# Low parts of the weights on VectorE alone, item 0's products in another order, an earlier start of the decoding, and the spare loop inside a conditional

## The chip, the cores and the metric

One core of a Trainium2 chip runs the whole program. The metric is the device time of one execution in microseconds, as the median of several runs. Engines are named as the profile names them: PE (TensorE), PEld (its weight loads), DVE (VectorE), ACT (ScalarE), POOL (GpSimd), SP (SyncE, which here issues the DMAs of weights).

## What is computed

Three layers follow each other: a block-sparse attention, a mixture of eight experts of which every token takes one, and a gated feed-forward block.

```python
x = attn(q, k, v)                       # (1536, 512): 2 x 768 tokens, 8 heads of 64
logits = x @ w_gate + modality_bias[modality_id]
e_idx = argmax(logits, axis=1)          # one of E = 8 experts for each token
for e in range(E):
    mask = e_idx == e
    h = maximum(x[mask] @ w1[e], 0.0)   # w1[e]: 512 x 1024
    out[mask] = gate_w[mask] * (h @ w2[e])   # w2[e]: 1024 x 512
g = out @ g2w                           # 512 x 1536
y = (silu(g) * (out @ v2w)) @ o2w       # o2w: 1536 x 512
```

The matrices of the feed-forward block come as 64-bit floating point numbers, all others as 32-bit.

## The kernel before

**Products in three parts.** Every float32 operand of a large product is written as a high part (float32 rounded to the format that PE multiplies, an ACT copy) and a low part (the operand minus its high part, a subtraction). `mm3` multiplies high by high, low by high and high by low: three matmuls, lines 802 to 804. For a weight tile, `split_w` makes both parts: line 788 on ACT makes `wh`, line 789 on the engine `eng` makes `wl`. A weight tile is 128x1024 (512 KB), and there are 8 for each item of work: four of w1 (`hidden`) and four of w2 (`project`).

**Items.** Tokens are sorted by expert on the chip, and the experts' work is cut into five items of fixed size, `KIND = "TQSQP"`: 3, 4, 1, 4 and 2 blocks of 128 tokens. Each item takes 4 steps with w1 and 4 with w2, and in each step the split of the tile three steps ahead (`WB`) is issued first, and the raw load of the tile three beyond that (`RB`). Both the raw tiles and the parts have three buffers: a raw tile's buffer comes free when its `wl` has been made, a part's buffer when the matmuls with it are done. Experts with more tokens than their item holds would go through a spare loop at line 1324, which runs `n_over` times.

**Who makes `wl`.** A list `DVES` (line 903) gives VectorE every second tile of item 0 and of the item of one block; the rest goes to POOL. In all, POOL makes 32 of the 40 tiles and VectorE 8.

**Item 0** runs while the routing of the later items is worked out on VectorE with many short instructions (`route`, `route_where`, `route_items`). Lines 1086 to 1113 fix the order by hand. PSUM has banks T (3), S (2), P (1) and V (2). `hidden` puts each half of its result in a T bank, ACT makes its high part `hh` (line 819) and VectorE its low part `hl` (line 822), which frees the bank. The low parts of `hidden_0(2)` are held back (`later`) until the routing of item 1 is done.

**Decoding.** The 64-bit weights are decoded on VectorE with five integer instructions for each half tile (lines 1200 to 1210, 128x512), then split: ACT makes the high part (line 1219), POOL the low part (line 1220). `decode` is a generator, and `bg_step(n)` runs n of its steps between other work. The first six halves are started at item 3 (`j == NS - 2`), the others inside the feed-forward block, which needs 36 in all.

All engines work through their instructions in the order of the program; nothing is reordered at run time.

Of the kernel before, what the change touches and what calls it, by code (L numbers as in the profile page):

```python
# [7 lines left out]
F32 = mybir.dt.float32  # L8
F32R = mybir.dt.float32r
BF16 = mybir.dt.bfloat16  # L10
I32 = mybir.dt.int32
ACTF = mybir.ActivationFunctionType
ALU = mybir.AluOpType
# [6 lines left out]
def sparse_attention_moe_swiglu_kernel(  # L20
# [45 lines left out]
    IT = 256  # L66
# [24 lines left out]
    def bank(tag):  # L91
        t = ps.tile([128, 512], F32, tag=tag, bufs=BANKS[tag], name="ps_" + tag)
        return t
# [709 lines left out]
        nc.tensor.matmul(out=out_, lhsT=ah, rhs=bl, start=False, stop=False)  # L803
        nc.tensor.matmul(out=out_, lhsT=al, rhs=bh, start=False, stop=stop)  # L804

    def hidden(c, x, w, later=None):
        n = x[0].shape[2]
        hh = pl["h"].tile([128, 2, n], F32R, tag="hh", name="hh")
        hl = pl["h"].tile([128, 2, n], F32R, tag="hl", name="hl")
        per = 512 // n  # L810
        for f0 in range(0, 2, per):
            p = bank("T")[:, 0:per * n].rearrange("p (f c) -> p f c", f=per)
            for f in range(f0, f0 + per):
                sl = slice(128 * f, 128 * f + 128)
                for kk in range(KD):
                    mm3(p[:, f - f0, :], w[0][:, kk, sl], w[1][:, kk, sl], x[0][:, kk, :], x[1][:, kk, :], kk == 0,
                        kk == KD - 1)
            fs = slice(f0, f0 + per)
            nc.scalar.activation(out=hh[:, fs], in_=p, func=ACTF.Relu)  # L819

            def low(p=p, fs=fs):
                nc.vector.scalar_tensor_tensor(out=hl[:, fs], in0=p, scalar=0.0, in1=hh[:, fs].bitcast(F32),  # L822
                                               op0=ALU.max, op1=ALU.subtract)

            if later is None:
                low()
            else:
                later.append(low)
        return hh, hl
# [69 lines left out]
    n_load = [0]  # L899
    n_split = [0]  # L900


    DVES = [i for i, (wn, j, c) in enumerate(preps) if (KIND[j] == "S" or i < 2 * NC1) and i % 2]

    def load_to(n):
        while n_load[0] < min(n, len(preps)):
            wn, j, c = preps[n_load[0]]
# [5 lines left out]
    def split_to(n, limit=None):  # L913
        limit = len(preps) if limit is None else limit
        while n_split[0] < min(n, limit):
            key = preps[n_split[0]]
            load_to(min(n_split[0] + RB, limit))
            ready[key] = split_w(pl["wc"], loaded.pop(key), nc.vector if n_split[0] in DVES else nc.gpsimd)
            n_split[0] += 1
        load_to(min(n_split[0] + RB, limit))  # L920

# [152 lines left out]
    split_to(2, 2 * NC1)  # L1074
    st_x(NT - 1)

    def hidden_0(c, later=None):
        split_to(c + WB, 2 * NC1)
        hs.append(hidden(c, x, ready.pop(("w1", 0, c)), later))

    def project_0(c, split=True):
        if split:
# [16 lines left out]
    adv(6)  # L1099
    for fn in later:  # L1100
        fn()
    hidden_0(3)
    yp = [y_banks(CT, "S")]
    project_0(0, False)
    while rg:
        adv(1000)
    xs = gather(pl["xg"], *idx_of(1))
    rg.append(route_items(2, NI))
    project_0(1)
    adv(6)  # L1110
    scale_x(xs)
    while rg:
        adv(1000)
    attn.close()
# [78 lines left out]
    def decode(wn, fb, i, pool):  # L1193
        r = r64.pop((wn, fb, i))
        shape = list(r.shape)
        w32 = r.bitcast(I32).rearrange("p a (b two) -> p a b two", two=2)
        lo, hi = w32[:, :, :, 0], w32[:, :, :, 1]
        a = dec_p.tile(shape, I32, tag="da", name="da")
        b = dec_p.tile(shape, I32, tag="db", bufs=1, name="db")
        nc.vector.tensor_scalar(out=a, in0=hi, scalar1=0x7FFFFFFF, scalar2=None, op0=ALU.bitwise_and)  # L1200
        nc.vector.tensor_scalar(out=b.bitcast(F32), in0=a.bitcast(F32), scalar1=T_LO, scalar2=T_HI, op0=ALU.max,
                                op1=ALU.min)
        yield
        nc.vector.tensor_scalar(out=a, in0=b, scalar1=3, scalar2=0x3FFFFFF8, op0=ALU.logical_shift_left,
                                op1=ALU.bitwise_and)
        yield
        nc.vector.scalar_tensor_tensor(out=b, in0=lo, scalar=29, in1=a, op0=ALU.logical_shift_right,  # L1207
                                       op1=ALU.bitwise_or)
        yield
        nc.vector.scalar_tensor_tensor(out=a, in0=hi, scalar=-2 ** 30, in1=b, op0=ALU.bitwise_and,  # L1210
                                       op1=ALU.bitwise_or)
        load64()
        yield
        if i == 0:
            whole = [128, 2, DM] if wn == "o" else [128, KD, 256]
            fw[wn, fb] = [pool.tile(whole, F32R, tag=wn + x, name=wn + x) for x in "hl"]
        part = (slice(None), slice(i, i + 1)) if wn == "o" else (slice(None), slice(None), slice(128 * i, 128 * i + 128))
        wh, wl = (t[part] for t in fw[wn, fb])
        nc.scalar.activation(out=wh, in_=a.bitcast(F32), func=ACTF.Copy)  # L1219
        nc.gpsimd.tensor_tensor(out=wl, in0=a.bitcast(F32), in1=wh.bitcast(F32), op=ALU.subtract)  # L1220

    def bg_step(n=1):
        while n and bg:
# [3 lines left out]
            except StopIteration:  # L1227
                bg.pop(0)

    store_y(0, yp[0], slice(0, CT), slice(0, CT))  # L1230
    yp.append(y_banks(CT, "T"))
    project_0(2)
    x = split_of(1, xs)
    project_0(3)
    store_y(1, yp[1], slice(0, CT), slice(0, CT))
    sexc = route_starts()

    def before(j):

        return min(NTOK, sum(128 * BLOCKS[kd] for kd in KIND[:j]))  # L1240

    done = 2 * NC1
    late = None
    for j in range(1, NS):
# [4 lines left out]
        n = 128 * BLOCKS[kd]  # L1249
        if not last:  # L1250
            xs = gather(pl["xg"], *idx_of(j + 1))
        if j == NS - 2:
            bg += [decode(wn, 0, i, fw_p) for wn in "gvo" for i in range(2)]
            load64()
            load64()
        hs, h1 = [], []
        for c in range(NC1):
            split_to(done + WB)
            w = ready.pop(("w1", j, c))
            if kd != "S":  # L1260
                hs.append(hidden(c, x, w))
            else:
                h1.append(hidden1(c, x, w))
                if c > 1:
                    hs.append(turn_h1(h1[c - 2]))
            if c == 0 and late is not None:
                store_y1(*late)
                late = None
            if c == NC1 - 1 and not last:
                scale_x(xs)  # L1270
            if c == 1 and j == 2:
                sorted_tokens(*tok_rows)
            bg_step(2)
            done += 1
        if last:
            break
# [2 lines left out]
        for c in range(NC1):  # L1279
            split_to(done + WB)  # L1280
            w = ready.pop(("w2", j, c))
            if c == 0 and kd == "S":
                yp = bank("S")
            elif c % 2 == 0 and kd != "S":
                yp = y_banks(n, "T" if c else "S")
            if kd != "S":
                project(c, hs, w, yp)
                if c % 2:
                    store_y(c // 2, yp, bass.ds(sa, n), bass.ds(sd, n))
            else:  # L1290
                project1(c, hs, w, yp)
                if c == 0:
                    hs += [turn_h1(h) for h in h1[2:]]
            bg_step(2)
            done += 1
            if c == 1:
                x = split_of(j + 1, xs)
            if c == 2 and j == 1:
                tok_rows = sorted_rows(sexc)
# [7 lines left out]
    for tag, d0, cols in (("S", 0, (0, 1)), ("S", 2, (0,)), ("V", 3, (1,))):  # L1307
        nd = len(cols)
        yp = bank(tag).rearrange("p (d c) -> p d c", d=2)[:, 0:nd]
        for c in (0, 1) if d0 == 0 else (2, 3):  # L1310
            if c not in ws:
                split_to(done + WB)
                done += 1
                ws[c] = ready.pop(("w2", NS - 1, c))
            project(c, hs, ws[c], [yp] * (1 if nd == 2 else 2), cols)
            bg_step(2)
        ds = slice(d0, d0 + nd)
        nc.scalar.activation(out=yh[:, ds, bass.ds(sa, IT)], in_=yp, func=ACTF.Copy)
        nc.vector.tensor_tensor(out=yl[:, ds, bass.ds(sd, IT)], in0=yp, in1=yh[:, ds, bass.ds(sd, IT)].bitcast(F32),
# [1 line left out]
    bg_step(100)  # L1321


    with tc.For_i(0, n_over, 1) as it:
        ii = pl["xg"].tile([128, 2], I32, tag="ii", name="ii")
        nc.vector.tensor_copy(out=ii, in_=idx[:, bass.ds(it * NB + NB * NS, 2)])
        e = nc.sync.value_load(tab[0:1, 0, bass.ds(it + NS, 1)], min_val=0, max_val=E - 1)
        xo = gather(pl["xg"], ii[:, 0:1], ii[:, 1:2])
        scale_x(xo)
        xo = split_x(pl["xg"], xo)  # L1330
        hs = [hidden(c, xo, split_w(pl["wc"], load_w(pl["raw"], e, "w1", c), nc.vector)) for c in range(NC1)]
        sa = nc.scalar.value_load(tab[0:1, 1, bass.ds(it + NS, 1)], min_val=0, max_val=NTOK)
        sd = nc.vector.value_load(tab[0:1, 1, bass.ds(it + NS, 1)], min_val=0, max_val=NTOK)
        for c in range(NC1):
            if c % 2 == 0:
                yp = y_banks(IT, "S")
            project(c, hs, split_w(pl["wc"], load_w(pl["raw"], e, "w2", c), nc.vector), yp)
            if c % 2:
                store_y(c // 2, yp, bass.ds(sa, IT), bass.ds(sd, IT))
    moe.close()  # L1340


# [88 lines left out]
```

## Time and profile before

| | us |
|---|---|
| median of 3 runs | 624.97 (623.2 to 626.79) |
| profiled execution, its own time | 623.85 |
| its span, first to last instruction | 622.1 |
| PE busy in the span | 575.0 (92%) |
| DVE busy | 381.9 (61%) |
| ACT busy | 212.3 (34%) |
| POOL busy | 194.5 (31%) |

The busy shares are means over stages with different limits: attention (to about 105 us), item 0 (to 163.06), items 1 to 4 (to 308.58) and the feed-forward block (from 313.98). [...]

### The profile page before, as it was taken

The numbers are of one execution on the slowest core, as the hardware profiler recorded it, in microseconds if no ns is written. First come the engines' busy times: TensorE is split into PE (matmuls) and PEld (weight loads), VectorE is DVE, ScalarE is ACT, GpSimd is POOL, SyncE is SP. The second block draws the span as 40 slices with busy tenths as digits, with TensorE's granted clock in tenths as the row PEclk, the third lists the DMA queues.
The fourth block names the chain that finished last, engine by engine and source line by source line (L and its number), as shares of the span: only waits on it lengthen the run. The fifth ranks groups of instructions, "written<-read, shape, count | busy, mean of one in ns | idle before, by whom it ended". The sixth has DMA issues, their size and how long they took to land.

```text
span 622.1 us, 9023 instructions
## 1 busy us (share of the span) xinstructions
PE 575.0 (92%) x3396; PEld 486.2 (78%) x3396; DVE 381.9 (61%) x688; ACT 212.3 (34%) x370; POOL 194.5 (31%) x252
## 2 busy tenths in 40 slices
PE   7969997977999979998689999999999999999995
PEld 6869986976888768888668888888888888888884
DVE  6557796657624654959304866947856875783333
ACT  5757844431432453344212343212121221221110
POOL 5572013215445637557400221201110210120025
PEclk8979998877999979999889999999999999999998
DMA  9999248324322637444100322212121220200013
GB/s 251 194 227 223 79 97 256 114 68 136 120 94 76 215 124 237 141 164 163 43 2 0 102 102 68 101 35 67 68 68 35 95 76 18 84 34 1 1 67 135
DMA packets 78270, 65.04 MB, mean 105 GB/s; under 512 B 25156, under 2 KB 73296, under 8 KB 78032
## 3 DMA queue, kind: packets, MB, share of 16 engines
q1 hardware_dynamic: 76144, 57.61, 32.6%
q0 software_dynamic: 2080, 6.82, 3.2%
q8 instruction: 28, 0.46, 0.3%
q14 instruction: 18, 0.15, 0.1%
HBM read 57.88 MB, written 6.35 MB: 103 GB/s over the span
## 4 chain that ended last, share of the span: by engine, by line
PE 48%; issue 1%; POOL 1%; POOLq 0%; DVE 0%
PE ps_T L802 11%; PE ps_T L804 11%; PE ps_T L803 11%; PE ps_S L803 3%; PE ps_S L802 3%; PE ps_S L804 3%; PE ps_V L804 1%; PE ps_P L802 1%; PE ps_V L803 1%; PE ps_V L802 1%; PE ps_P L803 1%; PE ps_P L804 1%; POOL out_dram L1381 1%; POOLq L1426 0%; POOL tk L1380 0%
## 5 line engine op out<-in xcount | busy, mean ns | idle before, releaser
L789 POOL TENSOR_TENSOR wl<-raw,wh 128x1024 fp32r<-128x1024 f32 x32 | 80.2, 2508 | 71.3 <-ACT wh L788 56.2
L1359 DVE TENSOR_TENSOR hv<-sg,ps_T 128x512 f32<-128x512 f32 x36 | 24.7, 686 | 83.2 <-PE ps_T L804 81.9
L802 PE MATMUL ps_T<-yh,gh 128*128 128x512 f32 x144 | 57.5, 399 | 5.4 <-issue 5.4
L1361 ACT ACTIVATE fh<-hv 128x512 fp32r<-128x512 f32 x36 | 22.8, 633 | 107.5 <-DVE hv L1359 107.5
L804 PE MATMUL ps_T<-yh,gl 128*128 128x512 f32 x144 | 57.1, 396 | 0.0
L803 PE MATMUL ps_T<-yl,gh 128*128 128x512 f32 x144 | 56.9, 395 | 0.0
L802 PE MATMUL ps_T<-yh,vh 128*128 128x512 f32 x144 | 56.8, 394 | 0.0
L804 PE MATMUL ps_T<-yh,vl 128*128 128x512 f32 x144 | 56.7, 394 | 0.0
L803 PE MATMUL ps_T<-yl,vh 128*128 128x512 f32 x144 | 56.3, 391 | 0.0
L1220 POOL TENSOR_TENSOR gl<-da,gh 128x512 fp32r<-128x512 f32 x12 | 15.6, 1302 | 127.4 <-ACT gh L1219 127.4
L802 PE MATMUL ps_T<-xh,wh 128*128 128x512 f32 (+2 forms) x128 | 47.0, 367 | 3.5 <-DVE hl L822 3.5
L804 PE MATMUL ps_T<-xh,wl 128*128 128x512 f32 (+2 forms) x128 | 46.6, 364 | 1.4 <-POOL wl L789 1.4
L788 ACT ACTIVATE wh<-raw 128x1024 fp32r<-128x1024 f32 x40 | 42.0, 1054 | 16.9 <-issue 4.0
L803 PE MATMUL ps_T<-xl,wh 128*128 128x512 f32 (+2 forms) x128 | 46.4, 363 | 0.0
L1357 ACT ACTIVATE sg<-ps_T 128x512 f32<-128x512 f32 x36 | 21.4, 594 | 59.6 <-PE ps_T L804 59.6
L1363 DVE TENSOR_TENSOR fl<-hv,fh 128x512 fp32r<-128x512 f32 x36 | 24.9, 693 | 25.2 <-ACT fh L1361 25.2
L802 PEld LDWEIGHTS ps_T<-yh,gh 128*128 128x128 f32 x144 | 27.4, 190 | 11.7 <-issue 5.6
L822 DVE SCALAR_TENSOR_TENSOR hl<-ps_T,hh 128x512 fp32r<-128x512 f32 (+1 forms) x28 | 17.8, 648 | 26.9 <-ACT hh L819 26.9
L804 PEld LDWEIGHTS ps_T<-yh,gl 128*128 128x128 f32 x144 | 27.3, 190 | 6.5
L803 PEld LDWEIGHTS ps_T<-yl,gh 128*128 128x128 f32 x144 | 27.4, 190 | 6.4
L1220 POOL TENSOR_TENSOR vl<-da,vh 128x512 fp32r<-128x512 f32 x12 | 16.2, 1354 | 51.2 <-ACT vh L1219 51.2
L1207 DVE SCALAR_TENSOR_TENSOR db<-r,da 128x512 int32<-128x512 int32 x36 | 31.9, 887 | 0.2
(300 smaller groups left out, 1428.7 us busy)
## 6 DMA issues: line engine op xcount, KB each, us to landing
raw<-in_moe_w_dram SPq DMA_DIRECT2D x40, 512.0 KB, 3.5
r<-in_moe_w_gate_dram SPq DMA_DIRECT2D x12, 512.0 KB, 3.6
r<-in_moe_w_val_dram SPq DMA_DIRECT2D x12, 512.0 KB, 3.6
r<-in_moe_w_out_dram SPq DMA_DIRECT2D x12, 512.0 KB, 3.1
ve<-in_v_dram SPq DMA_DIRECT2D x20, 192.0 KB, 5.2
ld<-in_k_dram SPq DMA_DIRECT2D x12, 256.0 KB, 5.6
ld<-in_q_dram SPq DMA_DIRECT2D x12, 256.0 KB, 3.8
x_d<-x SPq DMA_DIRECT2D x12, 256.0 KB, 5.1
```

What stands on the lines that cost most here:

```text
L788: nc.scalar.activation(out=wh, in_=src, func=ACTF.Copy)
L789: eng.tensor_tensor(out=wl, in0=src, in1=wh.bitcast(F32), op=ALU.subtract)
L802: nc.tensor.matmul(out=out_, lhsT=ah, rhs=bh, start=start, stop=False)
L803: nc.tensor.matmul(out=out_, lhsT=ah, rhs=bl, start=False, stop=False)
L804: nc.tensor.matmul(out=out_, lhsT=al, rhs=bh, start=False, stop=stop)
L822: nc.vector.scalar_tensor_tensor(out=hl[:, fs], in0=p, scalar=0.0, in1=hh[:, fs].bitcast(F32), op0=ALU.max, op1=ALU.subtract)
L1207: nc.vector.scalar_tensor_tensor(out=b, in0=lo, scalar=29, in1=a, op0=ALU.logical_shift_right, op1=ALU.bitwise_or)
L1220: nc.gpsimd.tensor_tensor(out=wl, in0=a.bitcast(F32), in1=wh.bitcast(F32), op=ALU.subtract)
L1357: nc.scalar.activation(out=sg, in_=gp_, func=ACTF.Silu)
L1359: nc.vector.tensor_tensor(out=hv, in0=sg, in1=vp_, op=ALU.mult)
L1361: nc.scalar.activation(out=hh, in_=hv, func=ACTF.Copy)
L1363: nc.vector.tensor_tensor(out=hl, in0=hv, in1=hh.bitcast(F32), op=ALU.subtract)
```

## The change

Five things change.

1. `DVES` is gone: VectorE makes `wl` of all 40 weight tiles, and the low parts of the 36 decoded halves too. In `decode` a `yield` is put ahead of that subtraction, so that a half takes five steps and a rest instead of four and a rest. POOL keeps its gathers and short work.
2. `hidden_0(3)` puts its second half in bank P instead of T (`tags="TP"`).
3. In item 0 the gather of item 1's tokens now stands ahead of `project_0(0)`; `project_0(2)`, `split_of(1)` and `project_0(3)` stand ahead of the matmuls that finish `route_items(2, NI)`; and both `store_y` come after all of it, that of the T banks first.
4. The decoding starts at item 1 (`j == 1`) instead of item 3, with 2 steps in each step of a four-block item, none in the one-block item, 1 in the two-block item (`STEPS`).
5. The spare loop stands inside `tc.If(n_over > 0, preferred_fallthrough_block=False)`.

```diff
-    def hidden(c, x, w, later=None):
+    def hidden(c, x, w, later=None, tags="TT"):
...
-            p = bank("T")[:, 0:per * n].rearrange("p (f c) -> p f c", f=per)
+            p = bank(tags[f0])[:, 0:per * n].rearrange("p (f c) -> p f c", f=per)
...
-    DVES = [i for i, (wn, j, c) in enumerate(preps) if (KIND[j] == "S" or i < 2 * NC1) and i % 2]
...
-            ready[key] = split_w(pl["wc"], loaded.pop(key), nc.vector if n_split[0] in DVES else nc.gpsimd)
+            ready[key] = split_w(pl["wc"], loaded.pop(key), nc.vector)
...
-    hidden_0(3)
-    yp = [y_banks(CT, "S")]
-    project_0(0, False)
+    hidden_0(3, tags="TP")
     while rg:
         adv(1000)
     xs = gather(pl["xg"], *idx_of(1))
+    yp = [y_banks(CT, "S")]
+    project_0(0, False)
     rg.append(route_items(2, NI))
     project_0(1)
     adv(6)
     scale_x(xs)
+    yp.append(y_banks(CT, "T"))
+    project_0(2)
+    x = split_of(1, xs)
+    project_0(3)
     while rg:
         adv(1000)
     attn.close()
...
-        nc.gpsimd.tensor_tensor(out=wl, in0=a.bitcast(F32), in1=wh.bitcast(F32), op=ALU.subtract)
+        yield
+        nc.vector.tensor_tensor(out=wl, in0=a.bitcast(F32), in1=wh.bitcast(F32), op=ALU.subtract)
...
-    store_y(0, yp[0], slice(0, CT), slice(0, CT))
-    yp.append(y_banks(CT, "T"))
-    project_0(2)
-    x = split_of(1, xs)
-    project_0(3)
-    store_y(1, yp[1], slice(0, CT), slice(0, CT))
+    for dp in (1, 0):
+        store_y(dp, yp[dp], slice(0, CT), slice(0, CT))
...
+    STEPS = {"Q": 2, "S": 0, "P": 1}
...
-        if j == NS - 2:
+        if j == 1:
             bg += [decode(wn, 0, i, fw_p) for wn in "gvo" for i in range(2)]
...
-            bg_step(2)
+            bg_step(STEPS[kd])
...
-    with tc.For_i(0, n_over, 1) as it:
+    with tc.If(n_over > 0, preferred_fallthrough_block=False):
+        with tc.For_i(0, n_over, 1) as it:
```

On DVE the end of item 0 is issued in another order. The rows go from the end of `route_items(2, NI)` to `route_starts`; `xs` are item 1's gathered tokens, scaled here, `xl` their low parts, `yl` the low parts of item 0's result.

```order
 L756 TENSOR_SCALAR xs<-xs 128x512 x4
-L542 CAST idx<-ps_V 128x76
-L853 TENSOR_TENSOR yl<-ps_S,yh 128x384 x2
+L789 TENSOR_TENSOR wl<-raw,wh 128x1024
 L771 TENSOR_TENSOR xl<-ps_V,xh 128x512
 L771 TENSOR_TENSOR xl<-ps_P,xh 128x512
 L771 TENSOR_TENSOR xl<-ps_V,xh 128x512
 L771 TENSOR_TENSOR xl<-ps_P,xh 128x512
+L789 TENSOR_TENSOR wl<-raw,wh 128x1024
+L542 CAST idx<-ps_V 128x76
 L853 TENSOR_TENSOR yl<-ps_T,yh 128x384 x2
+L853 TENSOR_TENSOR yl<-ps_S,yh 128x384 x2
```

The reading of the last indices (`idx`, which waits for PE) moved behind `xl`, two more `wl` stand in the row, and the low parts of the S banks are now made last, just ahead of `route_starts`.

On DVE in item 1, in the row from the second w2 step to the sorting of the tokens (`r_sp` is its first instruction), this stands now; before, `xl` of item 2 followed `yl` at once, and `r_sp` followed `xl`.

```order
L853 TENSOR_TENSOR yl<-ps_S,yh 128x512
L1222 TENSOR_TENSOR gl<-da,gh 128x4x128
L1201 TENSOR_SCALAR da<-r_2438 128x512
L1202 TENSOR_SCALAR db<-da 128x512
L1205 TENSOR_SCALAR da<-db 128x512
L781 TENSOR_TENSOR xl<-ps_V,xh 128x512
L789 TENSOR_TENSOR wl<-raw,wh 128x1024
L1208 SCALAR_TENSOR_TENSOR db<-r_2438,da 128x512
L1211 SCALAR_TENSOR_TENSOR da<-r_2438,db 128x512
L1138 TENSOR_TENSOR r_sp<-sc_205,h_211 128x84
```

Six instructions of the decoding and one `wl` have come between `yl` and the sorting.

## Rows read from the trace of the kernel before

**Rows 1.** Stages: start:end, length, busy us of each engine, clock, DMA share, GB/s.

```profile
126.50:163.06 36.56, 27.30 (x174) 26.61 (x173) 19.70 (x42) 8.57 (x14) 12.13 (x8) 0.81 0.32 102
...
207.70:231.55 23.85, 18.69 (x145) 17.17 (x144) 15.71 (x22) 12.45 (x18) 9.31 (x5) 0.86 0.53 173
...
278.10:308.58 30.48, 25.41 (x193) 24.59 (x191) 22.48 (x20) 11.33 (x17) 18.95 (x9) 0.94 0.35 116
...
313.98:606.00 292.02, 292.02 (x1259) 237.27 (x1260) 181.96 (x275) 67.50 (x114) 44.23 (x39) 1.00 0.17 55
```

**Rows 2.** Timeline of PE: start, length, instruction, and idle time before it with releaser.

```profile
130.06 0.69 PE L802 MATMUL ps_T<-xh,wh 128*128 128x384 f32 x1 [3.53 <-DVE hl L822]
...
148.75 1.49 PE L540 MATMUL ps_V<-bo,a 128*128 128x76 bf16 x21 [4.59 <-DVE bo L534]
...
158.38 0.66 PE L768 MATMUL ps_P<-ident,xs 128*128 128x128 f32 x4 [1.14 <-DVE xl L771]
...
222.56 0.58 PE L804 MATMUL ps_S<-wh,hl 128*128 128x256 f32 x1 [2.08 <-DVE hl L871]
...
232.95 0.50 PE L804 MATMUL ps_T<-xh,wl 128*128 128x512 f32 x1 [0.78 <-POOL wl L789]
...
296.11 0.39 PE L804 MATMUL ps_S<-hh,wl 128*128 128x256 f32 x1 [2.41 <-POOL wl L789]
...
313.98 0.79 PE L802 MATMUL ps_T<-yh,gh 128*128 128x512 f32 x1 [5.40 <-issue]
```

**Rows 3.** Stretches right after four of these idles, columns as in group 1.

```profile
130.06:135.97 5.91, 5.91 (x19) 5.91 (x19) 2.56 (x4) 1.44 (x2) 0.00 (x0) 0.50 0.35 115
148.75:153.15 4.40, 4.40 (x33) 4.40 (x33) 2.79 (x7) 1.82 (x3) 0.73 (x1) 0.52 0.67 232
158.38:163.06 4.68, 4.68 (x29) 4.68 (x29) 1.23 (x2) 1.88 (x3) 2.37 (x1) 1.00 0.01 4
296.11:299.71 3.60, 3.60 (x17) 3.60 (x18) 3.56 (x4) 0.00 (x0) 2.47 (x1) 0.53 0.00 0
```

**Rows 4.** The page's costliest groups: busy us, mean ns, idle before.

```profile
L789 POOL TENSOR_TENSOR wl<-raw,wh 128x1024 fp32r<-128x1024 f32 x32 | 80.2, 2508 | 71.3 <-ACT wh L788 56.2
...
L788 ACT ACTIVATE wh<-raw 128x1024 fp32r<-128x1024 f32 x40 | 42.0, 1054 | 16.9 <-issue 4.0
```

**Rows 5.** Line 789 on DVE: duration ns as minimum/median/maximum, first and last start.

```profile
L789 DVE TENSOR_TENSOR wl<-raw,wh x8: 1210/1225/2505, 110.1 to 222.8; 128x1024 fp32r<-128x1024 f32 x8
```

**Rows 6.** Timeline of DVE, single instructions from item 0 to the end of item 4.

```profile
129.33 0.21 DVE L534 TENSOR_TENSOR bo<-r_sc,code 128x48 bf16<-128x48 f32 x1
...
141.68 0.69 DVE L514 TENSOR_TENSOR r_lt<-cs,kk__208 128x513 bf16<-128x513 f32 x1
...
145.09 2.47 DVE L531 TENSOR_TENSOR r_sc<-kc,r_sm 128x76 f32<-128x76 f32 x1
...
148.62 1.67 DVE L756 TENSOR_SCALAR xs<-xs 128x512 f32<-128x512 f32 x4
...
170.05 1.28 DVE L822 SCALAR_TENSOR_TENSOR hl<-ps_T,hh 128x512 fp32r<-128x512 f32 x2
...
244.91 0.43 DVE L1204 TENSOR_SCALAR da<-db 128x512 int32<-128x512 int32 x1
...
293.89 2.45 DVE L1204 TENSOR_SCALAR da<-db 128x512 int32<-128x512 int32 x1
...
309.03 0.43 DVE L1319 TENSOR_TENSOR yl<-ps_V,yh 128x256 f32 x1 [2.45 <-ACTq L1324]
```

**Rows 7.** Timeline of POOL: the first gather of item 1, and two low parts.

```profile
140.33 0.99 POOL L749 DMA_INDIRECT xs<-x_d,idx  x1 [12.64 <-DVE idx L542]
...
293.53 5.05 POOL L789 TENSOR_TENSOR wl<-raw,wh 128x1024 fp32r<-128x1024 f32 x2
```

**Rows 8.** DMA from 308.6 to 314.2 us: GB/s in 40 slices, queue q8.

```profile
GB/s 0 0 0 0 0 0 0 117 0 0 0 0 0 0 0 0 0 0 0 0 0 0 0 0 0 0 0 0 0 0 0 117 0 0 0 0 0 0 0 0
...
q8 instruction: 2, 0.03, 2.5%
```

More of the change, by code (lines that the diff above doesn't have):

```diff
@@ L1075, in sparse_attention_moe_swiglu_kernel, with hidden_0 @@
     st_x(NT - 1)
-    def hidden_0(c, later=None):
+    def hidden_0(c, later=None, tags="TT"):
         split_to(c + WB, 2 * NC1)
-        hs.append(hidden(c, x, ready.pop(("w1", 0, c)), later))
+        hs.append(hidden(c, x, ready.pop(("w1", 0, c)), later, tags))
     def project_0(c, split=True):
@@ L1293, in sparse_attention_moe_swiglu_kernel @@
                     hs += [turn_h1(h) for h in h1[2:]]
-            bg_step(2)
+            bg_step(STEPS[kd])
             done += 1
@@ L1315, in sparse_attention_moe_swiglu_kernel @@
             project(c, hs, ws[c], [yp] * (1 if nd == 2 else 2), cols)
-            bg_step(2)
+            bg_step(STEPS["P"])
         ds = slice(d0, d0 + nd)
@@ L1321, in sparse_attention_moe_swiglu_kernel @@
     bg_step(100)
-    with tc.For_i(0, n_over, 1) as it:
[L1325 to L1339, printed above, removed]
+    with tc.If(n_over > 0, preferred_fallthrough_block=False):
+        with tc.For_i(0, n_over, 1) as it:
+            ii = pl["xg"].tile([128, 2], I32, tag="ii", name="ii")
+            nc.vector.tensor_copy(out=ii, in_=idx[:, bass.ds(it * NB + NB * NS, 2)])
+            e = nc.sync.value_load(tab[0:1, 0, bass.ds(it + NS, 1)], min_val=0, max_val=E - 1)
+            xo = gather(pl["xg"], ii[:, 0:1], ii[:, 1:2])
+            scale_x(xo)
+            xo = split_x(pl["xg"], xo)
+            hs = [hidden(c, xo, split_w(pl["wc"], load_w(pl["raw"], e, "w1", c), nc.vector)) for c in range(NC1)]
+            sa = nc.scalar.value_load(tab[0:1, 1, bass.ds(it + NS, 1)], min_val=0, max_val=NTOK)
+            sd = nc.vector.value_load(tab[0:1, 1, bass.ds(it + NS, 1)], min_val=0, max_val=NTOK)
+            for c in range(NC1):
+                if c % 2 == 0:
+                    yp = y_banks(IT, "S")
+                project(c, hs, split_w(pl["wc"], load_w(pl["raw"], e, "w2", c), nc.vector), yp)
+                if c % 2:
+                    store_y(c // 2, yp, bass.ds(sa, IT), bass.ds(sd, IT))
     moe.close()
```

## The prediction

> **What bounds the kernel now.** I read the stages first, then PE's timeline with what ended its idle times, then the queues of the engines named there. In the feed-forward block PE is busy for 292.02 of 292.02 us at clock 1.00 [rows 1]: nothing that takes work from another engine shortens it, so whatever the change brings comes before 313.98 us. There PE stands in four places. In item 0, from 126.50 to 163.06, it is busy for 27.30 of 36.56 us, and part of that at the low clock. The one-block item has 18.69 of 23.85, item 4 has 25.41 of 30.48, and between item 4 and the feed-forward block there is an idle of 5.40 us [rows 1, 2]. The reader is to see that three engines are named as releasers: DVE (the routing, ahead of 130.06 and 148.75), POOL (`wl`, ahead of 232.95 and 296.11), and nobody ("issue", ahead of 313.98) [rows 2].
>
> An idle has a second price. After those of 3.53, 4.59 and 2.41 us the clock row shows 0.50, 0.52 and 0.53 for the next 5.91, 4.40 and 3.60 us; after the idle of 1.14 it shows 1.00 [rows 2, 3]. Work at 0.50 takes twice as long, so these stretches lost 2.95, 2.1 and 1.7 us.
>
> **Item 0: 10.0 us gained.** PE's work in the stage at full clock is 27.30 less 2.95 less 2.1, or 22.25 us. To this come the idles that remain.
> First, the second half of `hidden_0(3)` no longer waits for the T bank whose `hl` stands behind the routing: bank P is free. It took four us of the low-clock stretch (12 of its 19 matmuls), so about 2.0, and ends at 128.5. The matmuls of L540 for item 1 still need `bo`, which DVE ends at 129.54 [rows 6]. DVE has one `wl` more ahead of that chain, but no POOL subtraction beside it; a short instruction there can be stretched as at 145.09, where 128x76 elements took 2.47 us. I let both cancel: idle 1.0.
> Second, the index copy for item 1 now stands behind four `hl` (0.64 each at most) and a `wl` of 1.23 [rows 5, 6], so gathers start at about 133.3 instead of 140.33 [rows 7]; in the trace their data were there 8.3 us after the first start, as nothing waited at 148.62 [rows 6], so by 141.6. On DVE follow two `wl`. The second needs the buffer that `project_0(0)` frees: L540 to 130.2, then its 24 matmuls to 134.4 (292.02 us for 1259 matmuls of 512 columns [rows 1] is 0.232 each, for 384 columns 0.174, so 4.2 a step), then `wh` 1.05 [rows 4] and `wl` 1.23, 136.7. Then the routing from L514 to `xs`, 6.94 us in the trace [rows 6], less 2.3 if its L531 takes 0.2 instead of 2.47: 141.3. `xs` 1.67: 143.0. PE ends `project_0(2)` at 142.8; with the gather's bound and a little slack I put an idle of 1.0 here.
> Third, the last transpose waits for `xl` behind a `wl`, as it did at 158.38: 1.3.
> Fourth, the idle of 4.59 us goes, since L540 for the later items now follows `project_0(3)`.
> The stage then takes 22.25 and 3.3, or 25.55 us, 11.0 less. One us is given back in item 1: there the first `hl` ran at 170.05, 7.0 us after the item began [rows 6], and with its 1.28 just in time for the fourth half step at 8.4. Now two `yl` of the S banks and a `wl` come ahead, less the contended part of `route_starts`. Bounds: 5 (the clock falls once, and gathers land late), 12 (no idle but 1.0 and no stall).
>
> **The four-block items: 0.** A step of 24 matmuls at 0.232 is 5.6 us of PE. DVE's load in a w1 step is `wl` 1.23, two `hl` 1.28 and two steps of decoding. A half tile is three instructions of 0.43 and three of two operands, for which I take 0.64, that of `hl` at the same size [rows 6] (bounds 0.43 and, stretched, 2.45); 3.2 us in five steps, so 1.3 in two. Together 3.8, covered by PE's 5.6. DVE's in-order wait for `wh` costs nothing: `wh` starts when PE ends a step, and `hl` is due half a step later. SP's raw loads are released by `wl` as before; the first 64-bit loads go out ahead of tile 13 instead of in item 3. POOL's gathers stand behind no `wl` any more. The 0.78 us at 232.95 goes.
>
> **The one-block item: 0.8 lost, so 0 with the 0.78.** At the end of item 1 DVE has 4.6 us more ahead of its next `wl`: the decoding and one `wl` among `yl`, `xl` and the sorting. That is late for the first tiles, whose buffers release the raw loads of the last. DVE makes it up: its own `wl` no longer alternates with one of 2.5 us on POOL [rows 4], and none is stretched to 2.505 [rows 5]. I take `hl`, on which PE waited at 222.56 [rows 2], as 0.8 late. Bounds: 3 lost (all but 1.6 of the 4.6 is kept), 2.5 gained (the idle of 2.08 goes).
>
> **Item 4: 6.8 gained.** Idle 5.07 (30.48 less 25.41 [rows 1]) and 1.7 of low clock. POOL's queue was the cause: two `wl` took 5.05 us there [rows 7], and DVE's decoding beside them was stretched, 2.45 for what took 0.43 at 244.91 [rows 6]. After the change the 30 steps of the first six halves fit in the 32 of items 1 and 3, so DVE has per step of 2.8 us (256 columns, half of 5.6) only a `wl` and an `hl`, 1.9. Bounds 5 and 7.6.
>
> **The conditional: 2.9 gained.** DVE's last subtraction ends at 309.46 [rows 6], so PE could begin some 0.3 later; it began at 313.98. In between queue q8 fetched instructions twice, at 309.6 and 312.9 (the eighth and the thirty-second slice of 0.14 us) [rows 8]. In the program before, a loop that runs no times jumps over the body to an exit block, in which each engine waits for all others, and from it on; with the conditional there is one jump, over the same body, and no exit block. I read one fetch as one jump and keep the first: PE begins at about 311.1. Bounds: 0.5, and 5.7, where both fetches go and with them 1.4 us of low clock behind the idle (as at 296.11).
> [...]
>
> **The feed-forward block: 0.** DVE gets 30 more subtractions of 0.64, 19 us on 181.96 of 292.02 [rows 1], and loses the stretching by POOL.
>
> **Sum.** 10.0 + 0 + 6.8 + 2.9 = 19.7. The profiled execution took 623.85, 1.1 below the median of the runs: 623.85 - 19.7 = 604.2, and I say **604**.
>
> **Rivals.**
> - DVE is late where POOL was free to wait: item 0 gives only 5 to 7 and the one-block item loses 3. For it speaks that DVE works in order, with the routing behind each `wl`; against it, that DVE is idle for 8 of 23.85 us there [rows 1]. Then 623.85 - (6 - 3 + 6.8 + 2.9) = 611.
> - The conditional frees the whole idle, and an idle or two of item 0 are shorter: 623.85 - (11 + 0 + 6.8 + 5.7) = 600.
> - The conditional does nothing, as both jumps cost a fetch: 604.2 + 2.9 = 607.
> - Slower: DVE becomes the bound of the four-block items. It does so from 5.6 us a step on, where two steps of decoding cost 3.1 instead of 1.3. With one such instruction at 2.45 and `wl` at its maximum of 2.505 [rows 5, 6] a step needs 7.1, 1.5 more than PE; over 16 steps 24 us, which outweighs the 19.7: 628. Against it: what stretched DVE were POOL's subtractions, and POOL has none left there.
> - Nothing moves (each idle is replaced by one on DVE as long): 624.
>
> **How the numbers follow.** Chances: forecast 0.62, DVE late 0.17, whole idle freed 0.10, conditional void 0.06, slower 0.03, nothing 0.02. All but the last two are faster by over 0.5%, which is about what a measurement of this kernel can tell from no change (3 us): faster 0.95, same 0.02, slower 0.03. The range takes the bounds of item 0, the one-block item and the conditional together, not all at their ends: 598 to 612; below and above remain 2 in 10.
>
> **What will show it.** Right: no PE idle over 1.5 us between 126 and 160; item 1's first matmul at 152 to 154; decoding instructions of DVE at 0.43 in items 1 and 3; item 4 in 23 to 24 us at clock 1.00; one fetch on q8 at the end of item 4, and an idle of 2 to 3 us. Wrong: a clock of 0.5 in item 0 after idles named "DVE xs" or "DVE bo"; an idle over 3 us in the one-block item with "DVE wl"; two fetches after item 4; PE idles in the feed-forward block.

## The result, and the profile after

The changed kernel takes 604.01 us (median of 4 runs, 602.91 to 607.11), the kernel before 624.13 on the same chip. The ratio is 0.968, interval 0.963 to 0.973: faster by about 20 us. The profiled execution took 604.52, its span is 602.7.

The stages first, in the columns of [rows 1]: item 0 from the second half of `hidden_0(3)` on, then items 1 to 4, the idle, and the feed-forward block up to PE's last product. The clock is PE's granted one as a share of full speed, over the span 0.960 before and 0.978 now; in the feed-forward block of both traces products of 512 columns start 0.43 us apart where it is 0.50, and 0.23 apart where it is 1.00.

```profile
125.75:150.03 24.28, 22.55 (x173) 21.78 (x173) 19.10 (x48) 7.63 (x11) 5.09 (x4) 1.00 0.49 162
150.03:195.30 45.27, 44.94 (x201) 36.51 (x199) 35.01 (x71) 17.55 (x26) 5.16 (x5) 1.00 0.55 176
195.30:219.74 24.44, 17.99 (x146) 16.57 (x145) 19.32 (x33) 12.53 (x19) 1.89 (x2) 0.93 0.54 161
219.74:265.20 45.46, 45.46 (x207) 37.32 (x205) 27.71 (x40) 18.24 (x26) 0.00 (x0) 1.00 0.50 157
265.20:288.39 23.19, 23.19 (x193) 22.98 (x191) 13.12 (x15) 10.00 (x14) 0.00 (x0) 1.00 0.22 69
288.39:292.84 4.45, 0.00 (x0) 0.03 (x1) 0.43 (x1) 1.67 (x2) 0.19 (x1) 1.00 0.02 6
292.84:595.43 302.59, 301.40 (x1296) 244.17 (x1296) 179.92 (x311) 67.83 (x114) 10.98 (x19) 0.99 0.17 57
```

Three stages of before that have no row among those shown ahead of the prediction: item 0 from its first product on, item 1, and the feed-forward block up to PE's last product.

```profile
109.11:163.06 53.95, 44.69 (x283) 43.28 (x281) 31.13 (x72) 17.36 (x29) 17.59 (x11) 0.85 0.32 100
163.06:207.70 44.64, 44.64 (x197) 36.43 (x197) 21.47 (x47) 15.53 (x22) 23.87 (x13) 1.00 0.34 114
313.98:614.87 300.89, 300.89 (x1296) 244.06 (x1296) 186.55 (x281) 67.50 (x114) 50.45 (x50) 1.00 0.17 57
```

| stage | before | after | gained | forecast |
|---|---|---|---|---|
| up to the second half of `hidden_0(3)` | 126.53 | 125.75 | 0.78 | 0 |
| item 0 from there | 36.53 | 24.28 | 12.25 | 11.0 |
| item 1 | 44.64 | 45.27 | -0.63 | -1.0 |
| one-block item | 23.85 | 24.44 | -0.59 | -0.8 |
| item 3 | 46.55 | 45.46 | 1.09 | 0.8 |
| item 4 | 30.48 | 23.19 | 7.29 | 6.8 |
| idle ahead of the feed-forward block | 5.40 | 4.45 | 0.95 | 2.9 |
| feed-forward block on PE | 300.89 | 302.59 | -1.70 | 0 |

The 126.53 is where the idle of 3.53 begins [rows 2]. With the tail behind PE (7.23 and 7.27) this is 19.4, the difference of the spans. The first row says little: in a second profile of the changed kernel item 0 began at 106.84 instead of 108.03.

The timeline of PE after: idles that are left, and new ones.

```profile
128.62 0.74 PE L540 MATMUL ps_V<-bo,a 128*128 128x4 bf16 x24 [0.59 <-DVE bo L534]
...
144.52 0.65 PE L768 MATMUL ps_P<-ident,xs 128*128 128x128 f32 x4 [1.14 <-DVE xl L771]
...
158.97 0.51 PE L802 MATMUL ps_T<-xh,wh 128*128 128x512 f32 x1 [0.33 <-DVE hl L822]
...
197.76 0.39 PE L802 MATMUL ps_T<-wh,xh 128*128 128x256 f32 x1 [0.84 <-DVE yl L853]
...
201.31 0.36 PE L802 MATMUL ps_T<-wh,xh 128*128 128x256 f32 x1 [1.27 <-DVE h L861]
...
211.00 0.58 PE L804 MATMUL ps_S<-wh,hl 128*128 128x256 f32 x1 [0.82 <-DVE hl L871]
...
292.84 0.73 PE L802 MATMUL ps_T<-yh,gh 128*128 128x512 f32 x1 [4.45 <-issue]
...
348.60 0.50 PE L802 MATMUL ps_T<-yh,vh 128*128 128x512 f32 x1 [1.19 <-ACT sg L1358]
```

Of the waits for `wl` on POOL none is left, and the clock of item 0 and of item 4 is 1.00. The idles of 3.53, 4.59 and 2.41 are gone; that ahead of the block is not. In the one-block item the wait for `hl` is shorter (0.82, it was 2.08), and two new ones stand ahead of it. Another new one stands at 348.60.

The instructions of DVE that were stretched take their short times now: line 531 had taken 2.47, line 1204 (now 1205) 2.45 and line 789 up to 2.505 us [rows 5, 6]. Over the whole span DVE is busy for 380.3 us, and for 381.9 before, although it makes 68 subtractions more (32 `wl` and 36 halves); POOL's busy time falls from 194.5 to 67.6. DVE's timeline in item 0:

```profile
139.16 0.23 DVE L531 TENSOR_TENSOR r_sc<-kc,r_sm 128x76 f32<-128x76 f32 x1
140.45 1.67 DVE L756 TENSOR_SCALAR xs<-xs 128x512 f32<-128x512 f32 x4
```

Two of its lines over the whole span, minimum, median and maximum in ns:

```profile
L789 DVE TENSOR_TENSOR wl<-raw,wh x40: 1215/1224/1226, 102.1 to 280.8; 128x1024 fp32r<-128x1024 f32 x40
...
L1205 DVE TENSOR_SCALAR da<-db x36: 417/426/430, 160.3 to 540.9; 128x512 int32<-128x512 int32 x36
```

### The profile page after: what moved, and what is told of

It is laid out like the page before. It is cut to its first block, busy times and chain, and to the rows that moved or that the text cites. A ratio compares the mean times of both kernels' runs of the same rounds, so it can differ in the third digit from the quotient of the medians.

```text
span 602.7 us, 8908 instructions
## 1 busy us (share of the span) xinstructions
PE 568.4 (94%) x3396; PEld 479.9 (80%) x3396; DVE 380.3 (63%) x756; ACT 212.3 (35%) x370; POOL 67.6 (11%) x184
## 4 chain that ended last, share of the span: by engine, by line
PE 47%; DVE 2%; POOL 1%; issue 1%; ACT 0%; POOLq 0%; DVEq 0%
PE ps_T L802 11%; PE ps_T L804 11%; PE ps_T L803 11%; PE ps_S L803 2%; PE ps_S L802 2%; PE ps_S L804 2%; PE ps_V L804 1%; PE ps_P L802 1%; PE ps_V L803 1%; PE ps_V L802 1%; PE ps_P L803 1%; PE ps_P L804 1%; POOL out_dram L1382 1%; DVE db L1208 0%; DVE da L1211 0%
## 5 line engine op out<-in xcount | busy, mean ns | idle before, releaser
L789 DVE TENSOR_TENSOR wl<-raw,wh 128x1024 fp32r<-128x1024 f32 x40 | 48.8, 1222 | 16.7 <-ACT wh L788 16.2
L802 PE MATMUL ps_T<-xh,wh 128*128 128x512 f32 (+2 forms) x124 | 45.0, 363 | 0.3 <-DVE hl L822 0.3
L1382 POOL DMA_INDIRECT out_dram<-acc,tk x12 | 11.9, 989 | 295.1 <-DVE acc L1377 293.5
L803 PE MATMUL ps_T<-xl,wh 128*128 128x512 f32 (+2 forms) x124 | 44.5, 359 | 0.0
L804 PE MATMUL ps_T<-xh,wl 128*128 128x512 f32 (+2 forms) x124 | 44.5, 359 | 0.0
L802 PEld LDWEIGHTS ps_T<-yh,vh 128*128 128x128 f32 x144 | 27.0, 188 | 7.6 <-ACT sg L1358 1.6
L804 PEld LDWEIGHTS ps_T<-yh,vl 128*128 128x128 f32 x144 | 27.0, 187 | 6.4
L803 PEld LDWEIGHTS ps_T<-yl,vh 128*128 128x128 f32 x144 | 27.0, 187 | 6.3
```

The source lines that it names most:

```text
L789: eng.tensor_tensor(out=wl, in0=src, in1=wh.bitcast(F32), op=ALU.subtract)
L802: nc.tensor.matmul(out=out_, lhsT=ah, rhs=bh, start=start, stop=False)
L1382: st = nc.gpsimd.indirect_dma_start(out=out, in_=acc[n], in_offset=None, out_offset=bass.IndirectOffsetOnAxis(ap=tk[:, 0:1], axis=0))
```

## The experiments

The kernel before had medians of 623.5, 623.0 and 622.6 us beside the three groups of runs, each group on another chip; ratios are to it. The changed kernel, run once more in the last group, took 603.68 (0.969, 0.966 to 0.972).

**Where the time came from: part 1 alone, parts 2 and 3 alone.**

```
-    DVES = [...]
...
-   split_w(..., nc.vector if n_split[0] in DVES else nc.gpsimd)
+   split_w(..., nc.vector)
...
-   nc.gpsimd.tensor_tensor(out=wl, ...)      # in decode
+   yield
+   nc.vector.tensor_tensor(out=wl, ...)
```

> The kernel before with part 1 of the change alone: VectorE makes all low parts. Theory (item 4's idle came from POOL's queue and from POOL's subtractions beside DVE): item 4 in about 24 us instead of 30.5, item 0 1 to 2 us shorter since the routing is no longer stretched (its instruction of 2.47 us takes 0.2), feed-forward block 1 to 2 us longer by DVE's added work: about 617 us. Rival (the early start of the decoding is what frees item 4): item 4 keeps at least 4 of its 5 us of idle, since DVE now has wl and decoding there: 622.

613.56 us, ratio 0.985 (0.980 to 0.990). Windows of it, item 0 from its first product and item 4:

```profile
107.49:158.25 50.76, 43.56 (x283) 42.15 (x282) 31.56 (x77) 17.35 (x29) 10.50 (x10) 0.90 0.36 115
...
270.53:295.35 24.82, 23.87 (x193) 23.13 (x191) 21.55 (x33) 11.98 (x18) 0.00 (x0) 1.00 0.39 127
```

The one idle of PE in item 4, in its timeline:

```profile
291.01 0.39 PE L804 MATMUL ps_S<-hh,wl 128*128 128x256 f32 x1 [0.84 <-DVE wl L789]
```

Item 4 falls from 30.48 to 24.82 although all its `wl` and the late decoding now share DVE: the rival falls. Item 0 is 3.2 shorter (53.95 to 50.76), more than the 1 to 2 expected. The time is 3.4 below the 617 expected. The windows of the other stages place two more gains, the one-block item (23.85 to 22.18) and item 3 (46.55 to 45.46), and a loss of 2.5 in the feed-forward block (300.89 to 303.40).

Parts 2 and 3, the order of item 0 alone, with POOL's `wl` as before:

```
-    hidden_0(3)
+    hidden_0(3, tags="TP")
...
+    project_0(2)
+    x = split_of(1, xs)
+    project_0(3)
```

> The kernel before with parts 2 and 3 alone: bank P for the second half, and item 0's products in the new order; POOL makes 32 of 40 wl as before. Theory (the order gives most of item 0, but the routing is still stretched by POOL, so xs comes 2 to 4 us late): item 0 in 27 to 30 us instead of 36.5, time 616. Rival (the order alone gives all that was measured, 24.3 us): 612. Rival (without part 1 the gathers stand behind wl on POOL and xs is so late that the clock falls again): item 0 in 32 or more, 620.

622.87 us, ratio 1.002 (0.998 to 1.006): nothing gained, against every theory stated. Its windows, item 0 from its first product, and item 1:

```profile
106.08:152.81 46.73, 41.18 (x283) 38.76 (x281) 32.43 (x69) 16.48 (x26) 17.94 (x11) 0.96 0.37 116
152.81:202.59 49.78, 46.49 (x201) 37.66 (x199) 25.26 (x50) 16.51 (x24) 23.33 (x12) 0.97 0.32 103
```

PE's timeline, the longest idle in each of the two:

```profile
143.04 1.61 PE L768 MATMUL ps_V<-ident,xs 128*128 128x128 f32 x4 [2.54 <-DVE xs L756]
...
164.70 0.73 PE L802 MATMUL ps_T<-xh,wh 128*128 128x512 f32 x1 [3.29 <-DVE hl L822]
```

DVE's timeline, the slowest instructions of the routing:

```profile
133.78 5.23 DVE L517 TENSOR_TENSOR mtab<-r_lt 128x456 bf16<-128x456 bf16 x1
...
155.87 2.76 DVE L557 TENSOR_TENSOR r_mu<-mtab,r_u 128x480 f32<-128x480 bf16 x1
...
159.80 3.10 DVE L565 TENSOR_TENSOR sc<-sc 128x21 f32<-128x21 f32 x5
```

POOL's timeline at the time of the first:

```profile
133.98 4.71 POOL L789 TENSOR_TENSOR wl<-raw,wh 128x1024 fp32r<-128x1024 f32 x2
```

Item 0 is 7.2 us shorter, as I expected, but item 1 is 5.1 longer: `hl` stands behind the longer row of DVE work that part 3 puts ahead of it, and POOL's subtractions draw that row out. Lines 557 and 565, here 2.76 and 3.10, had taken 0.66 and 1.05 in the kernel before. In item 0 one instruction of 0.46 us lasts 5.23, as long as two `wl` on POOL beside it. So parts 2 and 3 pay little without part 1: 3.2 and 7.2 - 5.1 apart, 12.0 - 0.6 together. Of those 2.1 the median shows 0.6; in this profile the feed-forward block took 1.5 us longer than before, with a longer stretch at the low clock behind the idle (0.50 over the block's first four us, 0.64 before).

**The stretching by itself.** POOL gets useless work beside the last 24 weight tiles of the changed kernel; nobody waits for its results.

```
+            if n_split[0] >= 4 * NC1:
+                for kk in range(KD):
+                    part = ready[key][0][:, kk, :].bitcast(F32)
+                    nc.gpsimd.tensor_tensor(out=spare, in0=part, in1=part, op=ALU.subtract)
```

> The changed kernel with useless work on POOL: beside each weight tile of the last three items POOL subtracts the tile's high part from itself, 1024 columns in four pieces, into a tile that nobody reads. Nothing on another engine waits for it. Theory (POOL's subtractions stretch VectorE's instructions beside them): decoding and other short instructions of DVE are stretched from 0.43 to 1.5 or 2.5 us where they fall beside it, wl to 2 us or more, and PE's idles grow in the one-block item and in items 3 and 4: 3 to 8 us slower, 607 to 612. Rival (item 4's idle before was only POOL's queue, wl made late, and the sharing is harmless): 604 to 605, DVE's durations unchanged.

607.80 us, ratio 0.977 (0.971 to 0.982). Windows of the one-block item and of items 3 and 4:

```profile
193.82:223.42 29.60, 20.74 (x145) 19.31 (x144) 25.01 (x36) 13.02 (x19) 26.72 (x29) 0.77 0.50 161
223.42:268.88 45.46, 45.46 (x206) 37.35 (x205) 33.41 (x40) 18.02 (x26) 34.45 (x42) 1.00 0.50 158
268.88:292.08 23.20, 23.20 (x193) 22.98 (x191) 14.03 (x15) 10.02 (x14) 19.51 (x24) 1.00 0.23 78
```

PE's two longest idles in the one-block item, in its timeline:

```profile
198.24 0.39 PE L802 MATMUL ps_T<-wh,xh 128*128 128x256 f32 x1 [2.81 <-DVE yl L853]
...
214.43 0.58 PE L804 MATMUL ps_S<-wh,hl 128*128 128x256 f32 x1 [2.98 <-DVE hl L871]
```

DVE's timeline there, while POOL works through the useless pieces without a pause from 200.2 to 230.6:

```profile
209.05 0.41 DVE L871 TENSOR_TENSOR hl<-ps_V,hh 128x256 fp32r<-128x256 f32 x1
209.38 3.12 DVE L756 TENSOR_SCALAR xs<-xs 128x512 f32<-128x512 f32 x4
212.41 1.63 DVE L789 TENSOR_TENSOR wl<-raw,wh 128x1024 fp32r<-128x1024 f32 x1
```

In the profile items 1, 3 and 4 lose nothing and the one-block item 5.2 us, 29.60 against 24.44; by the medians the loss is 3.8 to 4.1. There `xs` takes 3.12 instead of 1.67 and `wl` 1.63 instead of 1.22, while `hl`, one of whose inputs is in PSUM, keeps its 0.41; PE then waits 2.98 for the `hl` behind them, against 0.82 in the changed kernel.

PE's wait for `yl` at the start of the item is 2.0 longer as well: the useless work begins at 184.8, and up to `yl` five instructions of DVE take 1.9 more than in the changed kernel (4.88 for 3.00). PE's idles in the item together grow by 2.4; the rest of the 5.2 is work at a lower clock (0.77, not 0.93). The gathers, which are also queued behind the useless work, don't explain it: DVE stood idle ahead of none of these. In items 3 and 4 DVE is busier too (33.41 against 27.71 in item 3), but PE's steps cover it.

So beside the same work of POOL `xs` and `wl` were stretched and `hl` was not, with the three durations above; why these and not that one is not shown. How much an instruction is stretched varies in the trace: of the `wl` beside the useless work one took 1.22, as long as without it.

**Part 4 undone.**

```
-    STEPS = {"Q": 2, "S": 0, "P": 1}
+    STEPS = {"Q": 2, "S": 2, "P": 2}
...
-        if j == 1:
+        if j == NS - 2:
```

> The changed kernel with part 4 undone: the first six halves are decoded in items 3 and 4 again, two steps in each. Theory (VectorE alone frees item 4, and the early start adds little: with VectorE alone and late decoding item 4 took 24.8 us, against 23.2 in the changed kernel): item 4 about 1.6 us longer, item 1 and the one-block item 0.6 and 2 us shorter, since the decoding of item 1 no longer delays the one-block item: 603 to 604 us, no change. Rival (the early decoding is worth its 2 to 3 us): 606 or more, with item 4 at 26 or more.

603.29 us, ratio 0.967 (0.964 to 0.971), against 603.68 and 604.01 with part 4. The windows of the one-block item and of item 4:

```profile
195.54:218.64 23.10, 18.93 (x145) 17.53 (x144) 16.49 (x26) 12.35 (x18) 1.90 (x2) 0.85 0.52 168
...
264.10:288.91 24.81, 23.86 (x193) 23.12 (x191) 21.55 (x33) 11.99 (x18) 0.00 (x0) 1.00 0.37 121
```

1.6 lost in item 4, 1.3 gained in the one-block item: the early start moves 1.5 us from one place to another. The two waits for `yl` and `h` at the start of the one-block item are gone here. Of the 7.29 in item 4, 5.7 belong to part 1 and 1.6 to part 4.

**Part 2 undone.**

```
-    hidden_0(3, tags="TP")
+    hidden_0(3)
```

> The changed kernel with part 2 undone: both halves of the last product with w1 in item 0 go to T banks. Theory (the second half then waits for the held-back hl again, some 3 us as with VectorE alone, and the clock falls behind it): an idle of 3.2 us, 1.5 to 2 us of low clock, less what it saves at the next wait for bo (0.6): item 0 in 46 instead of 42.0 us from its first product on, 608. Rival (the wait moves onto bo and xs, which are late anyway): 605.

608.83 us, ratio 0.977 (0.973 to 0.981): 5 us slower than the changed kernel. In the profile item 0 takes 45.44 from its first product, against 42.00 and 41.84 in two profiles with bank P, so 3.5 of the 5 are placed; the rest is not resolved. PE's timeline:

```profile
129.59 0.69 PE L802 MATMUL ps_T<-xh,wh 128*128 128x384 f32 x1 [3.17 <-DVE hl L822]
```

**The conditional.** First the spare loop written plainly again.

```
-    with tc.If(n_over > 0, preferred_fallthrough_block=False):
-        with tc.For_i(0, n_over, 1) as it:
+    with tc.For_i(0, n_over, 1) as it:
```

> The changed kernel with the spare loop written plainly again, without the conditional. Theory (the conditional is worth the difference of the two idles ahead of the feed-forward block, 5.40 less 4.45 us): 605.0 us, 0.95 slower than the changed kernel, and an idle of 5.4 on PE with two fetches on q8. Rival (the 2.9 us of the prediction, which something else at this place took back): 606.9. Rival (the conditional is worth nothing): 604.0, idle 4.45.

604.94 us, ratio 0.972 (0.967 to 0.977): 0.9 to 1.3 above the changed kernel, and the idle is 5.40. That is the 0.95 of the profile, though the times alone would not tell it from nothing. The profiles bear it out: with the plain loop the idle is 5.40, 5.40, 5.40 and 5.10 in the four that have it, and with the conditional over the long body between 4.07 and 4.45 in all six. Then the loop left out altogether:

```
-    with tc.If(n_over > 0, preferred_fallthrough_block=False):
...
```

> The changed kernel with the spare loop and its conditional left out; with these inputs the loop runs no times, so nothing that is computed here is missing. Theory (what is left of the idle is the jump and its fetches): PE then waits only for the last yl, which ends 0.9 us after PE's last product, so an idle of about 1.0 instead of 4.45, no low clock behind it (1.75 us less), no fetch just there: 604.0 - 3.45 - 1.75 = 598.8. Rival (the next code has to be fetched with or without a jump): idle 2 to 3 and the low clock stays, 602. Rival (the idle is something else, such as the table load of 1.28 us on ACT): 604.

596.82 us, ratio 0.958 (0.953 to 0.963): 7 us less than the changed kernel. PE's timeline, the last product of item 4 and the first of the block:

```profile
286.60 0.28 PE L804 MATMUL ps_V<-hh,wl 128*128 128x256 f32 x1
286.72 0.40 PE L802 MATMUL ps_T<-yh,gh 128*128 128x512 f32 x1
```

The window of the four us from there:

```profile
286.72:290.72 4.00, 4.00 (x20) 3.21 (x19) 0.42 (x1) 2.27 (x3) 0.00 (x0) 1.00 0.00 0
```

No idle at all, not even the 1.0 that I expected for the last `yl`: that ends at 287.75, and the first products, which don't read it, begin at 286.72. The clock stays at 1.00; in the changed kernel the four us behind the idle have 0.57. The block takes PE 301.0 us, and 302.6 in the changed kernel, the idle at `sg` in both: 1.6 us of low clock. (In the second profile of the changed kernel it is 2.7, behind an idle of 4.07.) So the place is worth 4.45 and 1.6, or 6 us by the profile, 7 by the medians.

What it is in the jump, the next run tells: conditional and loop are kept, but the body is short.

```
             xo = gather(pl["xg"], ii[:, 0:1], ii[:, 1:2])
             scale_x(xo)
             xo = split_x(pl["xg"], xo)
-            hs = [hidden(c, xo, ...
...
```

> The changed kernel with the conditional and the spare loop in place, but a body that holds only the index copy, the gather, the scaling and the split of the tokens (8 transposes on PE instead of some 200 instructions); the matmuls of the body are left out, and with these inputs it never runs. Theory (the idle is the jump over the body to code that isn't loaded): with a short body the target is near, no fetch must be waited for, idle 0.5 to 1.5 us and clock 1.00 behind it, 599 to 600. Rival (the idle is the price of the conditional's join or of its branches, whatever the distance): idle 4 to 4.5, 604. Rival (each branch costs a fetch, near or far): the same.

597.82 us, ratio 0.959 (0.955 to 0.962). PE's timeline, the first product of the block:

```profile
288.76 0.47 PE L802 MATMUL ps_T<-yh,gh 128*128 128x512 f32 x1 [0.87 <-ACTq L1324]
```

The window of the four us from there:

```profile
288.76:292.76 4.00, 4.00 (x17) 3.26 (x18) 0.01 (x1) 1.69 (x2) 0.00 (x0) 1.00 0.01 4
```

The DMA from 287 to 293 us, in 40 slices of 0.15 us:

```profile
GB/s 0 0 0 0 0 0 0 0 0 0 0 0 0 0 0 0 0 0 109 0 0 0 0 0 0 0 0 0 0 0 0 0 0 0 0 0 0 0 0 0
...
q8 instruction: 1, 0.02, 1.0%
```

The same branches over a short body leave 0.87 us, a wait that other instructions release, and the one fetch comes after PE has begun (289.7 against 288.76). The 3.6 us between 4.45 and 0.87 are the price of the long body. The same view of the changed kernel, from 288 to 294:

```profile
GB/s 0 0 0 0 0 0 0 0 0 109 0 0 0 0 0 0 0 0 0 55 0 0 0 0 0 0 0 0 0 0 0 0 0 109 0 0 0 0 0 0
...
q8 instruction: 2, 0.03, 2.2%
```

One fetch of q8 at 289.4, the other at 293.0, behind PE's start at 292.84 (the middle one is of another queue). In the kernel before, the second comes at 312.9, ahead of the start at 313.98 [rows 2, 8].

That PE waits for one of these fetches is not shown: the second one lands behind PE's start in the changed kernel, no row tells what PE does between the first, at 289.4, and 292.84, and in the run without the loop q8 fetches once too, at 286.4, with no idle of PE behind it.

**The idle at 348.60.** More steps of decoding in the first round of the block:

```
                 h2.append(gv(tg, f, fw["g", fb], fw["v", fb]))
-                bg_step(2)
+                bg_step(4 if fb == 0 else 2)
```

> The changed kernel with four steps of decoding instead of two after each product pair in the first round of the feed-forward block. Theory (the idle of 1.2 us there, absent in the kernel before, comes from the added step of each half: 30 steps are wanted, 24 are called, and the 6 left run in one burst, with ACT's oh ahead of its sg): the idle disappears, 604.0 - 1.2 = 602.8. Rival (the idle comes from VectorE's added subtractions as such, wherever they stand): it stays or moves, 604.0.

602.34 us, ratio 0.966 (0.964 to 0.969), 1.3 to 1.7 below the changed kernel, and the idle is gone. ACT's timeline of the changed kernel shows how it arose:

```profile
343.33 0.63 ACT L1220 ACTIVATE oh<-da 128x512 fp32r<-128x512 f32 x1 [2.50 <-DVE da L1211]
347.43 0.63 ACT L1220 ACTIVATE oh<-da 128x512 fp32r<-128x512 f32 x1 [3.47 <-DVE da L1211]
347.97 0.58 ACT L1358 ACTIVATE sg<-ps_T 128x512 f32<-128x512 f32 x1
```

`oh`, the high part of a decoded half, waits 3.47 for DVE, and `sg` is queued behind it, though PE ended the product that it reads at 341.92, two products earlier; PE needs the bank that `sg` frees. The added `yield` gives a half five counted steps, and six halves 30; the first round calls 24, and the rest runs in one burst.

**A version without the jump.** The feed-forward block follows item 4 at once. Behind it stands the conditional, which with spare items would run the loop and then the whole block again; with these inputs it is skipped. The second run adds the steps of the last experiment.

```
     moe.close()
+    feed_forward()
+    with tc.If(n_over > 0, preferred_fallthrough_block=False):
+        open_moe()
+        open_h()
+        with tc.For_i(0, n_over, 1) as it:
...
+        moe.close()
...
+        feed_forward()
```

> The changed kernel with the spare loop moved behind the feed-forward block: the block follows item 4 at once, and a conditional at the very end would, if there were spare items, work through them and run the whole block again; with these inputs it is skipped. Theory (the jump costs PE 4.4 us only where PE has work behind it, and at the end the last stores run 7 us longer than PE): no idle ahead of the block, full clock, 604.0 - 4.45 - 1.75 = 597.8, at most 1 us lost at the end. Rival (the jump of POOL or SP at the end, and the wait of all engines there, come on top of the stores): 600 to 602.

> Both of the last two ideas: the spare loop behind the feed-forward block, and four steps of decoding in its first round. Theory (the two savings are at different places and add up): 597.8 - 1.2 = 596.6. Rival (without the idle ahead of the block VectorE has less time in hand and the decoding is late elsewhere): 598 or more, with a new idle on PE named sg or one of the decoded tiles.

599.54 us (0.963, 0.960 to 0.967) and 599.87 (0.964, 0.961 to 0.967), against 603.68 for the changed kernel in the same group: both beat it by about 4 us. PE goes from item 4 to the block without an idle, but at the end 2.5 us are lost. In PE's timeline of the first of them the last product ends 9.8 ahead of the end of the span, 597.1; in the changed kernel it is 7.3.

```profile
586.92 0.40 PE L804 MATMUL ps_V<-oh,fl 128*128 128x512 f32 x1
```

So the first theory was right on PE and wrong at the end (2.5 where I allowed 1). In the second run the idle at `sg` is gone and its block is 1.5 us shorter, but the median isn't lower: that the two savings add up is not shown. The case with spare items was not timed.

> The changed kernel once more, unaltered, on the same chip as the three others of this group, so that they are compared with it and not with another chip. Every theory expects 603 to 605 us, an idle of 4.4 us ahead of the feed-forward block and one of 1.2 in its second round.

603.68 us; the idles are 4.07 and 1.18.

## Why the prediction was right, and where not

That the time came out at 604 is in part luck, since errors cancelled: in the table above the terms of the conditional and of the feed-forward block fall short by 3.65 us, all others exceed the forecast by 3.4 together, 0.8 of it ahead of item 0's second half, where no gain was forecast. The two large terms, item 0 and item 4, were right in their mechanism.

- **Item 0: right in mechanism, 1.6 too small** (11.6 net of item 1 instead of 10.0). The idles that I kept were 1.0, 1.0 and 1.3; they are 0.59, none, and 1.14 (in the second profile 0.58, 0.57 and 1.14). `xs` came at 140.45 and not at 141.3, and was in time. Item 1 therefore began at 150.03, ahead of the 152 to 154 that I had named. I had let DVE's added `wl` cancel against the relief from POOL; the relief is larger, as the run with the order alone shows. The give-back in item 1 is 0.63, with 0.33 of it at the T bank as said. Work at clock 0.50 took some 1.8 times as long as at 1.00 (0.43 and 0.23 us, above), where I took twice.
- **Four-block items: right.** Decoding stays at 0.42 to 0.43 (line 1205, maximum 0.430 us), and the wait of 0.78 in item 3 is gone. The slower rival needed an instruction of 2.45 there; none exists without POOL's subtractions.
- **One-block item: right in size and cause, wrong in place**, 0.59 lost against 0.8. The early decoding is the cause: without it the item takes 23.10. But I took the `hl` at 222.56 as 0.8 later, and its wait fell from 2.08 to 0.82; PE waits for `yl` and `h` at the start instead, 0.84 and 1.27. The early decoding costs 1.3; that only 0.59 is lost is due to part 1, which alone shortens the item by 1.7.
- **Item 4: right**, 7.29 against 6.8, in 23.19 us at clock 1.00. POOL is the cause that was shown: PE waited for its `wl` [rows 2], and with DVE alone 5.7 of it go. That run ends POOL's queue and the stretching of DVE together. The stretching that I named beside the queue is real, but useless work on POOL cost this item nothing; whether it did with the decoding beside it is open.
- **The conditional: the step that failed.** "I read one fetch as one jump and keep the first" was an estimate of mine from the two fetches of before: there are still two fetches, and the idle is 4.45, not 2 to 3. The jump over the long body costs nearly all of it: 3.6 of the 4.45 go when the body is short. What the conditional removes from the plain loop is 0.95 us; that this is the exit block fits, but no run shows it by itself. Of the 2.9, 1.9 were not there. The 311.1 in the forecast doesn't follow from the fetches either: the first at 309.6, with the 1.1 us by which PE began behind the second, gives 310.7.
- **The feed-forward block: 0 forecast, 1.7 lost.** I counted DVE's added subtractions against its free time, which was enough, and missed that the added `yield` lengthens the row of steps beyond those called: 1.19. The other 0.5 is a longer stretch of low clock behind the idle, and that need not be an effect of the change: this stretch differs between executions of the changed kernel by as much as 1.1 us (PE busy for 301.40 and 302.52 in its two profiles).

## What to carry to other kernels

Work on POOL was paid for twice here, in its own time and in the stretching of VectorE: taking over 68 subtractions left VectorE no busier than before (380.3 us for 381.9). Give such work to the faster engine first (a `wl` took 1.22 us on VectorE, 2.51 on POOL), and reorder afterwards, since here the order alone gained nothing (622.87 us). Count the steps of background work against the calls that run them, when a step is added; what is left over runs in a burst, and whatever is queued behind it on another engine waits (PE for 1.19 us here). At a loop that runs no times PE stood for 4.45 us here, and for 0.87 with a short body: shorten the body, or put it where the engine that jumps has nothing behind it (599.54 us, against 603.68).

## What was not expected of the hardware

- At the skipped body PE was idle for 4.45 us when it is long and for 0.87 when it is short; behind idles of 4.45 and 4.07 us the low clock took 1.6 and 2.7 us.
- The stretch at clock 0.50 behind equal idles differed between executions: after 5.40 us of idle the first four us of the block had a granted clock of 0.64 before the change and 0.50 with the loop written plainly in the changed kernel.
- An idle of 0.87 us, in the run with the short body, left the clock at 1.00 for the next four us.
